# Maximum tiles paced by VectorE's work, one PSUM pool, first weights in pieces, and an output projection in program order

## The chip, the cores and the metric

The kernel runs on one core of one Trainium2 chip. The metric is device microseconds of one execution; the median of three runs of the kernel before is 1812.08 us. The engines are called as the profile calls them: PE (TensorE matmuls), PEld (its weight loads), DVE (VectorE), ACT (ScalarE), POOL (GpSimd), SP (SyncE, which issues DMAs).

## The reference

The kernel mixes, by a gate for each token, an attention block and a token-mixing MLP on the same input x of 2048 tokens and 640 channels:

```
q, k, v = split(x @ wqkv)                      # 32 heads of 20
a = softmax(q k^T / sqrt(20)) v  @ wo          # 2048 x 640
h = layernorm(x)                               # over channels
u = gelu(h^T @ w1 + b1)                        # 640 x 1728, over tokens
b = (u @ w2 + b2)^T                            # 2048 x 640
g = sigmoid(sum(x * gate_w, -1))
out = g * a + (1 - g) * b
```

All is float32. Products are made of a high part rounded for the fast matmul and a low part (`hi_lo`), three matmuls for one.

## The kernel before

The work is one program in five stages.

1. **q and k projections** (0 to 63 us). `qk_unit(m, w, q)` makes one tile of 128 output channels by 512 tokens with 15 matmuls into one PSUM tile and then evacuates it: the high part by ACT (`evh`), the low part by DVE (`evl`), and for some units a third copy by DVE (`kf`). The first weights (`wr0`) come in one DMA on ACT's queue, x in twenty pieces on SP's.
2. **v projections** (63 to 134 us), 32 units of 15 matmuls, evacuated by ACT (`vt`) and, in the first half, by DVE (`gs`, which also feeds the gate). Then the other q and k units (134 to 218 us), beside the splitting of the normalised rows (`h_split`) and loads of the next weight tile: at the first of a weight tile's four units ACT issues the load of the next one and, in its own order, waits for it in `load_w`.
3. **Token MLP** (218 to 746 us): `mlp` is a generator of 2592 steps, each one or two matmuls into a pair of half-width tiles. Beside its steps runs the **maximum stream**: for the softmax, the largest score of each query row is needed ahead of the exponentials, so all scores are made once with PE and only their maxima kept. For the first 8 head pairs (`s_diff`) halves of the keys are differenced, so that ACT (relu, `ov`) and DVE (`tensor_tensor_reduce`) share the work; for the rest (`s_raw`) DVE alone reduces every tile (`mx`). The stream takes 1082 tiles beside the MLP (1024 differenced, 58 raw), two at a time, spread evenly over the steps; what is left runs in the attention loop.
4. **Attention loop** (747 to 1721 us): 512 iterations, each with scores (`st`), exponentials on ACT (`p`) and the product with v on PE (`pv`). Its output `o_d` and the softmax sums `l_d` go to DRAM; `norm_steps` loads the sums, takes reciprocals on DVE and stores them, broadcast, to `r_d`.
5. **Output projection** (1722 to 1800 us): for each of 16 row tiles 24 matmuls over four of the five channel chunks, then in a second pass six matmuls for the last chunk, each pass evacuated by DVE into `oy`, which already holds the MLP's part.

The order on PE, and in stages 1 to 4 on ACT and DVE (from the MLP on also on POOL and SP), is the program's own order. In the output projection of the kernel before, only PE's order is fixed by the program (`ordered.close()` stands ahead of it); the other engines' is the scheduler's. In the MLP a small planner (`act`, `later_on`, `settle`, `force`) sets where ACT's work stands: each piece has a cost, a delay and a slack, and the earliest due comes first.

**PSUM** has 8 banks: the pool `four` (later `trio`, then `late`) gives four tiles in rotation (`st0` to `st3`) to `st_tile`, which the projections, the MLP and the output projection use; the rest belong to the maximum stream (`s`, `s3`, `pv`). In the attention loop the scores take one two-bank tile (`two`) and single ones (`one0`, `one1`, `s3`).

Of the kernel before, what the change touches and what calls it, by code (L numbers as in the profile page):

```python
# [10 lines left out]
OP = mybir.AluOpType  # L11
# [19 lines left out]
def gated_mix(ctx, tc, xT, x, wqk, wv0, wv1, wo, w1, w1t, b1, w2, b2, out):  # L31
# [303 lines left out]

    def load_x(q):
        for c in range(NC):
            raw = px.tile([P, 512], F32, tag="x", bufs=8, name=f"xr{c}_{q}")
            nc.sync.dma_start(raw, xT[c * P:(c + 1) * P, q * 512:(q + 1) * 512])
            hi_lo(xh[c][q], xl[c][q], raw, hi_eng=nc.scalar)  # L340
# [453 lines left out]

    def norm(h0, h1, at):
        loads, recips, stores = norm_steps(h0, h1)
        for n, f in enumerate(loads + recips + stores):
            if at is None:
                f()
            else:  # L800
                later[at if n == 0 else at + 10 + 2 * n] = f

    def pv_evac(p, qh, pv):
        ev = ap.tile([P, 512], F32, tag="oev", bufs=2, name=f"oev{p}_{qh}")
        nc.vector.tensor_copy(ev, pv)  # L805
        for j in range(2):
            h = 2 * p + j
            for c in range(2):
                r = 32 * (2 * j + c) + 11 * j
                cols = slice(qh * 1024 + c * 512, qh * 1024 + (c + 1) * 512)  # L810
                nc.gpsimd.dma_start(o_d[DH * h: DH * h + DH, cols], ev[r: r + DH, :])  # L811
                nc.gpsimd.dma_start(l_d[h: h + 1, cols], ev[r + DH: r + DH + 1, :])
        if qh == 1 and p in (7, 11, 13, 15):
            norm({7: 0, 11: 16, 13: 24, 15: 28}[p], 2 * p + 2, None if p == NP - 1 else 32 * p + 38)
# [23 lines left out]
    o_hl = {}  # L838

    def o_part(q, rows, k, n, tag, bufs, hi_eng, lo_eng):  # L840
        def t(name, dt=F32):
            return ap.tile([P, k, n], dt, tag=name + tag, bufs=bufs, name=f"{name}{tag}{q}")
        raw, rb, oh, ol = t("or"), t("rb"), t("oh", F32R), t("ol", F32R)
        cols = slice(q * n, (q + 1) * n)
        nc.sync.dma_start(raw, o_d[rows].rearrange("(c p) s -> p c s", p=P)[:, :, cols])
        nc.sync.dma_start(rb, r_v[rows].rearrange("(c p) s -> p c s", p=P)[:, :, cols])
        nc.vector.tensor_mul(raw, raw, rb)
        hi_lo(oh, ol, raw, hi_eng=hi_eng, lo_eng=lo_eng)
        return [(oh[:, i], ol[:, i]) for i in range(k)]

    def o_early(q, hi_eng=nc.scalar, lo_eng=nc.vector):
        o_hl[q] = o_part(q, slice(0, (NC - 1) * P), NC - 1, 256, "e", 2, hi_eng, lo_eng)

    def o_late(q):
        return o_part(q, slice((NC - 1) * P, D), 1, 512, "l", 4, nc.scalar, nc.vector)[0]
# [11 lines left out]
    def st_pair(g):  # L867
        ps = tp.tile([P, 2, 512], F32, tag="two", bufs=1, name=f"st{g}_0")
# [6 lines left out]
    def st_one(g, j):  # L875
        n = (2 * g + j) % 3
        ps = (psum if n == 2 else tp).tile([P, 512], F32, tag=("one0", "one1", "s3")[n], bufs=1, name=f"st{g}_1{j}")
# [6 lines left out]
    for p in range(NP):  # L884
# [3 lines left out]
        for it in range(32):  # L888
# [14 lines left out]
            if p == NP - 1 and it in (20, 26):  # L903
                o_early(it // 26, nc.gpsimd, nc.gpsimd)
# [25 lines left out]
    def a_mms(t, ps, ohl, cc, cs):  # L930
        passes = [z for k, (oh, ol) in zip(cs, ohl) for z in ((oh[:, cc], woh[k]), (oh[:, cc], wol[k]),
                                                              (ol[:, cc], woh[k]))]
# [4 lines left out]
        c = slice(t, t + 1)  # L937
        for i in range(2):
            nc.vector.scalar_tensor_tensor(tys[t][:, i], ps[i], g_t[:, c], tys[t][:, i], op0=OP.mult, op1=OP.add)  # L939

    last = []
# [59 lines left out]
```

## Time and profile before

| | |
|---|---|
| runs | 1811.72, 1812.08, 1812.80 us |
| profiled execution, own time | 1807.24 us |
| its span | 1804.9 us |
| PE busy | 1787.0 us (99%), 14978 matmuls |
| ACT busy | 1483.9 us (82%) |
| DVE busy | 1240.6 us (69%) |
| POOL busy | 641.8 us (36%) |
| mean granted PE clock | 0.997 |

The profile comes from one execution, so its rows are set against its own time of 1807.24 us, which is 4.84 us below the median of the runs. A row of the windows table gives a stretch of the span, the busy time and number of instructions of each engine in it, the granted clock and the DMA traffic. A row of the timeline gives start, duration, engine, line, operation, the names of output and inputs, and in brackets the idle time before it and what ended that. A row of the table of waits gives the total, the number and the longest. A row of the groups of instructions gives busy time, mean duration in ns, and idle time ahead.

### The profile page before, as it was taken

Reading aid. Unit: us, or ns where it says so; the run is one execution under the profiler, and the core shown is the slowest. Engines: PE = TensorE matmul, PEld = TensorE weight load, DVE = VectorE, ACT = ScalarE, POOL = GpSimd, SP = SyncE. Lnnn points to the kernel's source line nnn. Section 1 sums busy time; section 2 is a strip of 40 time slices with the busy share of each in tenths; the row PEclk is TensorE's granted clock in tenths of the full one; section 3 lists DMA queues with packets and bytes.
Section 4 is the critical chain, followed back from the end, with each engine's and each line's share of the span. In section 5 each row is a group of like instructions: output and inputs, shape, how many; then the busy total and the mean of one; then the engine's idle time right before and its main releaser. Section 6 shows DMA issues by size and latency. Waiting matters only on the chain. (4 is left out here: it accounts for less than half of the span.)

```text
span 1804.9 us, 39919 instructions
## 1 busy us (share of the span) xinstructions
PE 1787.0 (99%) x14978; PEld 1117.5 (62%) x14978; DVE 1240.6 (69%) x2407; ACT 1483.9 (82%) x2535; POOL 641.8 (36%) x898
## 2 busy tenths in 40 slices
PE   9999999999999999999999999999999999999998
PEld 7998799999999999533333333333333333333378
DVE  5303288899988888877767767676767677766136
ACT  4244378887888887699999999999999999999920
POOL 2113378788877777211110211121322121212210
PEclk9999999999999999999999999999999999999999
DMA  8657866556675564225222232052353332301463
GB/s 301 233 172 247 269 160 170 160 160 190 187 182 149 156 178 141 70 59 135 59 53 58 62 90 61 18 113 62 62 122 69 72 71 53 73 14 23 134 223 135
DMA packets 155666, 222.96 MB, mean 124 GB/s; under 512 B 65998, under 2 KB 92382, under 8 KB 152046
## 3 DMA queue, kind: packets, MB, share of 16 engines
q1 hardware_dynamic: 135472, 186.78, 38.2%
q0 software_dynamic: 15104, 23.01, 5.4%
q10 hardware_dynamic: 4896, 10.62, 1.8%
q8 instruction: 118, 1.93, 0.5%
q14 instruction: 76, 0.62, 0.1%
HBM read 165.43 MB, written 54.54 MB: 122 GB/s over the span
## 5 line engine op out<-in xcount | busy, mean ns | idle before, releaser
L205 DVE TENSOR_REDUCE mx<-s 128x1 f32<-128x512 f32 x1280 | 833.7, 687 | 288.9 <-PE s L199 225.1
L880 ACT ACTIVATE p<-st 128x512 f32<-128x512 f32 x1024 | 585.1, 659 | 0.0
L872 ACT ACTIVATE p<-st 128x1024 f32<-128x1024 f32 x512 | 553.8, 1082 | 1.3 <-PE st L865 0.7
L824 PE MATMUL pv<-p,v 128*32 128x512 f32 x4096 | 548.5, 605 | 0.1
L865 PEld LDWEIGHTS st<-qs_True,ks_True 62*128 62x128 f32 x2048 | 246.2, 185 | 434.9 <-ACT p L872 428.7
L865 PE MATMUL st<-qs_True,ks_True 62*128 62x512 f32 x2048 | 495.7, 446 | 1.8 <-ACT x L587 1.1
L199 PE MATMUL s<-ks_False,qs_False 60*128 60x512 f32 x1152 | 391.0, 398 | 4.5 <-ACT ov L214 2.9
L43 POOL TENSOR_TENSOR wl<-wr,wh 128x512 fp32r<-128x512 f32 x228 | 275.4, 1217 | 89.0 <-ACT wh L40 66.8
L224 DVE CUSTOM_DVE_ANT_0 ov<-s,ov 128x512 f32<-128x512 f32 x384 | 263.4, 687 | 38.6 <-PE s L199 24.9
L214 ACT ACTIVATE ov<-s 128x512 f32<-128x512 f32 x384 | 228.7, 597 | 73.0 <-PE s L199 61.9
L199 PE MATMUL s<-sk,sq 60*128 60x512 f32 x896 | 279.9, 394 | 0.0
L811 POOL DMA_DIRECT2D o_d<-oev x128 | 66.6, 521 | 590.4 <-DVE oev L805 587.9
L48 PE MATMUL y<-gh,wh 64*128 64x320 f32 x896 | 225.0, 309 | 0.0
L48 PE MATMUL u<-hl,wh 64*128 64x320 f32 x864 | 224.7, 307 | 0.0
L48 PE MATMUL u<-hh,wh 64*128 64x320 f32 x864 | 224.5, 307 | 0.0
L199 PEld LDWEIGHTS s<-ks_False,qs_False 60*128 60x128 f32 x1152 | 211.2, 185 | 14.7 <-DVE mx L205 6.7
L48 PE MATMUL y<-gl,wh 64*128 64x320 f32 x832 | 216.7, 307 | 0.0
L48 PE MATMUL y<-gh,wl 64*128 64x320 f32 x832 | 215.3, 306 | 0.0
L48 PE MATMUL u<-hh,wl 64*128 64x320 f32 x800 | 212.3, 307 | 0.0
L824 PEld LDWEIGHTS pv<-p,v 128*32 128x32 f32 x4096 | 83.1, 108 | 175.1 <-issue 162.6
L40 ACT ACTIVATE wh<-wr 128x512 fp32r<-128x512 f32 (+2 forms) x246 | 146.9, 600 | 52.7 <-DMA wr<-in_wqk_dram 22.5
L199 PEld LDWEIGHTS s<-sk,sq 60*128 60x128 f32 x896 | 166.3, 186 | 18.0
(130 smaller groups left out, 2441.3 us busy)
## 6 DMA issues: line engine op xcount, KB each, us to landing
wr<-in_w_dram SPq DMA_DIRECT2D x192, 256.0 KB
ks_True<-k_d SPq DMA_DIRECT2D x96, 160.0 KB
qs_True<-q_d SPq DMA_DIRECT2D x192, 80.0 KB
qs_False<-q_d SPq DMA_DIRECT2D x108, 80.0 KB
sk<-k_d SPq DMA_DIRECT2D x42, 160.0 KB
sq<-q_d SPq DMA_DIRECT2D x84, 80.0 KB
v_d<-vt SPq DMA_DIRECT2D x32, 168.0 KB
v<-v_d SPq DMA_DIRECT2D x16, 336.0 KB
```

The lines of the kernel that those rows point to most:

```text
L40: nc.scalar.activation(hi, src, AF.Copy)
L43: (lo_eng or nc.vector).tensor_sub(lo, src, hi.bitcast(F32))
L48: nc.tensor.matmul(ps[k], a[r], b[r], start=start, stop=stop)
L199: nc.tensor.matmul(ps, qs[half][r, t * P:(t + 1) * P], ks[r, kc * 512:(kc + 1) * 512], start=True, stop=True)
L205: nc.vector.tensor_reduce(mx[:, slot, j, t: t + 1], ps, axis=AX.X, op=OP.max)
L214: nc.scalar.activation(over[j, kc], ps, AF.Relu)
L224: nc.vector.tensor_tensor_reduce(ov, ps, ov, 1.0, -3.0e38, OP.add, OP.max, mx[:, slot, j, t: t + 1])
L811: nc.gpsimd.dma_start(o_d[DH * h: DH * h + DH, cols], ev[r: r + DH, :])
L824: nc.tensor.matmul(pv[r: r + 32, :], v_tiles[p][:, kt, 10 * j: 10 * j + 32], pt[j, c], start=(kt == 0), stop=(kt == NT - 1))
L865: nc.tensor.matmul(ps, ks[r, kt * P:(kt + 1) * P], qs[qh][r, c * 512:(c + 1) * 512], start=True, stop=True)
L872: nc.scalar.activation(pt, ps, AF.Exp, scale=SCALE)
L880: nc.scalar.activation(pt, ps, AF.Exp, scale=SCALE)
```

## The change

- `st_tile` gives the two halves of one two-bank tile (`two`) for every first and second call of four, and two single tiles (`one0`, `one1`) for the third and fourth. All PSUM tiles now come from one pool, and `four`, `trio` and `late` are gone, so the attention loop's tiles are the same as the earlier stages'.
- The warm-up takes 8 matmuls in another tile. The first weights come in five DMAs, all x loads of the first column are issued at once, and the splits of weights and x alternate.
- The maximum stream is paced by an estimate of DVE's work: 435 for a differenced tile, 640 for a raw one, 400 for each row tile that DVE normalises in the second half of the channels, from step 14 on. The splits of the first 8 weight chunks of the MLP have another delay and slack.
- The softmax sums are stored ahead of the outputs; the last normalisation's reciprocals and stores are placed in the output projection.
- The output projection is written in program order for all engines (`ordered.close()` at the end). From row tile 8 on, a tile takes all five chunks at once, and behind it stands the last chunk of the tile 8 rows earlier.

The core of the diff:

```diff
-    four = ExitStack()
-    banks = [four.enter_context(tc.tile_pool(name="four", bufs=1, space=PSUM))]
 
     def st_tile(shape, name):
         n = st_count[0] % 4
         st_count[0] += 1
-        return banks[0].tile(shape, F32, tag=f"st{n}", bufs=1, name=name)
+        if n == 0:
+            st_pair_of[0] = psum.tile([P, 2, 512], F32, tag="two", bufs=1, name=name)
+        if n < 2:
+            return st_pair_of[0][:, n, :shape[1]]
+        return psum.tile(shape, F32, tag=f"one{n - 2}", bufs=1, name=name)
...
-    wps = st_tile([P, 512], "warm_ps")
-    for i in range(10):
-        nc.tensor.matmul(wps, warm[:, :P], warm, start=(i == 0), stop=(i == 9))
-    raws = {0: w_dma(0), NC: w_dma(NC)}
-    w = {0: load_w(0, raws[0])}
-    load_x(0)
+    wps = s3_tile([P, 512], "warm_ps")
+    for i in range(8):
+        nc.tensor.matmul(wps, warm[:, :P], warm, start=(i == 0), stop=(i == 7))
+    wr0 = p1.tile([P, NC, P], F32, tag="xr", bufs=2, name="wr0")
+    for c in range(NC):
+        nc.scalar.dma_start(wr0[:, c], wqk[0][:, c])
+    xr0 = [x_dma(c, 0) for c in range(NC)]
+    raws = {NC: w_dma(NC)}
+    w = {0: tuple(q4([P, NC, P], F32R, f"w{n}0") for n in "hl")}
+    for c in range(NC):
+        hi_lo(w[0][0][:, c], w[0][1][:, c], wr0[:, c], hi_eng=nc.scalar)
+        x_split(c, 0, xr0[c])
...
-            act(lambda: w_split(j), 520, 0, 2200 * (j - k) - 4000)
+            act(lambda: w_split(j), 520, 4000 if j < 2 * AHEAD else 0, 2000 if j < 2 * AHEAD else 2200 * (j - k) - 4000)
...
+    FIRST = 14
+    U_STEPS = (FT - 1) * 48 + 32
+    DIFF, RAW, NORM = 435, 640, 400
+
+    def dve_work(k):
+        return DIFF * min(k, NDIFF * 128) + RAW * max(0, k - NDIFF * 128)
+
+    def dve_room(n):
+        norms = min(max((n - U_STEPS) / (NT * 40), 0), 1) * NT * NORM
+        return (dve_work(S_AHEAD) + NT * NORM) * (n + 1 - FIRST) / (STEPS - FIRST) - norms
...
-        while done + 2 <= S_AHEAD and done < S_AHEAD * (n + 1) / STEPS:
+        while done + 2 <= S_AHEAD and dve_work(done) < dve_room(n):
...
-    four.close()
-    trio = ExitStack()
-    tp = trio.enter_context(tc.tile_pool(name="trio", bufs=1, space=PSUM))
...
         if qh == 1 and p in (7, 11, 13, 15):
-            norm({7: 0, 11: 16, 13: 24, 15: 28}[p], 2 * p + 2, None if p == NP - 1 else 32 * p + 38)
+            h0 = {7: 0, 11: 16, 13: 24, 15: 28}[p]
+            if p == NP - 1:
+                last_norm.extend(norm_steps(h0, H))
+                last_norm[0][0]()
+            else:
+                norm(h0, 2 * p + 2, 32 * p + 38)
...
     pv_flush()
-    ordered.close()
     lps.close()
-    trio.close()
-    banks[0] = ctx.enter_context(tc.tile_pool(name="late", bufs=1, space=PSUM))
...
     for t in range(NT):
-        if t % 2 == 0 and t // 2 + 2 < NT // 2:
-            o_early(t // 2 + 2)
-        nc.sync.dma_start(tys[t].rearrange("p a b -> p (a b)"), y_d[t * P:(t + 1) * P, :])
-        if t in (4, 6, 8, 10):
-            last.append(o_late(t // 2 - 2))
-        ps = [st_tile([P, HALF], f"a{t}_{i}") for i in range(2)]
-        a_mms(t, ps, o_hl[t // 2], slice((t % 2) * P, (t % 2 + 1) * P), range(NC - 1))
-    for t in range(NT):
-        ps = [st_tile([P, HALF], f"b{t}_{i}") for i in range(2)]
-        a_mms(t, ps, [last[t // 4]], slice((t % 4) * P, (t % 4 + 1) * P), [NC - 1])
-        nc.scalar.dma_start(out[t * P:(t + 1) * P, :], tys[t].rearrange("p a b -> p (a b)"))
+        q = t // 2 + 2
+        if t % 2 == 0 and 2 < q < NT // 2:
+            e_high(q, ap if q % 4 < 2 else ep)
+        if t == 2:
+            for f in last_norm[2]:
+                f()
+            for n in (2, 0, 3, 1):
+                l_load(n)
+        for n in {NT // 2 - 2: (2, 0), NT // 2 + 1: (3, 1)}.get(t, ()):
+            l_high(n)
+        evacs = [a_tile(t, range(NC) if t >= NT // 2 else range(NC - 1))]
+        if t >= NT // 2:
+            evacs.append(a_tile(t - NT // 2, [NC - 1]))
...
+        for f in evacs:
+            f()
+        if t == 1:
+            for f in last_norm[1]:
+                f()
+    ordered.close()
```

How this moves instructions shows at three places. The first is PE's order where the first unit with the weights of m = 1 ends and its second begins. A row names the output tile, then the moving and the stationary operand; the number behind a name is the buffer's. Before:

```order
L54 MATMUL qk1_0_489<-xh4_0_117,wh1_351 128x512
L54 MATMUL qk1_0_489<-xl4_0_137,wh1_351 128x512
L54 MATMUL qk1_0_489<-xh4_0_117,wl1_352 128x512
L54 MATMUL qk1_1_515<-xh0_1_102,wh1_351 128x512
L54 MATMUL qk1_1_515<-xl0_1_122,wh1_351 128x512
L54 MATMUL qk1_1_515<-xh0_1_102,wl1_352 128x512
```

and in the changed kernel, at the same place:

```order
L54 MATMUL qk1_0_494<-xh4_0_114,wh1_357 128x512
L54 MATMUL qk1_0_494<-xl4_0_134,wh1_357 128x512
L54 MATMUL qk1_0_494<-xh4_0_114,wl1_358 128x512
L54 MATMUL qk1_0_494<-xh0_1_99,wh1_357 128x512
L54 MATMUL qk1_0_494<-xl0_1_119,wh1_357 128x512
L54 MATMUL qk1_0_494<-xh0_1_99,wl1_358 128x512
```

The order of the matmuls is the same; the second unit's output was a tile of its own and is now the same tile as the first unit's (its other half).

The second is ACT's order where the MLP begins: `wh` and `wtmp` are the high parts of MLP weight chunks, `wr` their raw loads, `ov` the relu of a differenced tile `s`. Before:

```order
L40 ACTIVATE evh_3_2174<-qk_3_2158 128x512
L40 ACTIVATE wtmp_1447<-wr_2128 128x512
L483 DMA wr_2188<-in_w_dram 128x512
L483 DMA wr_2190<-in_w_dram 128x512
L40 ACTIVATE wh_2196<-wr_2154 128x512
L214 ACTIVATE ov_0_0_1_0_2205<-s_0_0_1_0_2201 128x512
L214 ACTIVATE ov_0_0_1_2_2220<-s_0_0_1_2_2213 128x512
```

and now:

```order
L40 ACTIVATE evh_3_2163<-qk_3_2147 128x512
L40 ACTIVATE wtmp_1442<-wr_2117 128x512
L499 DMA wr_2176<-in_w_dram 128x512
L499 DMA wr_2178<-in_w_dram 128x512
L218 ACTIVATE ov_0_0_1_0_2219<-s_0_0_1_0_2215 128x512
L218 ACTIVATE ov_0_0_1_2_2234<-s_0_0_1_2_2227 128x512
L40 ACTIVATE wh_2244<-wr_2143 128x512
```

The split of the chunk that follows stood ahead of the first two relus and now stands behind them.

The third is PE's order near the MLP's end, among the raw maximum tiles `s`; `y` rows are the MLP's own matmuls, and `x2` marks two of them in one row. Before:

```order
L199 MATMUL s_0_4_1_0_13332<-ks_False,qs_False_11652 128x512
L199 MATMUL s_0_4_0_0_13335<-ks_False,qs_False_11652 128x512
L48 MATMUL y_14_0_13248<-gh_7_9786,wl_13139 128x320
L48 MATMUL y_14_1_13249<-gh_7_9786,wl_13139 128x320
L48 MATMUL y_14_0_13248<-gh_8_9986,wh_13180 128x320
L48 MATMUL y_14_1_13249<-gh_8_9986,wh_13180 128x320
L48 MATMUL y_14_0_13248<-gl_8_9987,wh_13180 128x320
L48 MATMUL y_14_1_13249<-gl_8_9987,wh_13180 128x320
L48 MATMUL y_14_0_13248<-gh_8_9986,wl_13181 128x320
L48 MATMUL y_14_1_13249<-gh_8_9986,wl_13181 128x320
L48 MATMUL y_14_0_13248<-gh_9_10186,wh_13180 128x320
L48 MATMUL y_14_1_13249<-gh_9_10186,wh_13180 128x320
```

and now, up to the next pair of tiles:

```order
L203 MATMUL s_0_4_1_0_13231<-ks_False,qs_False_11496 128x512
L203 MATMUL s_0_4_0_0_13234<-ks_False,qs_False_11496 128x512
L48 MATMUL y_14_0_13238<-gh_0_8147,wh_13095 128x320 x2
L48 MATMUL y_14_0_13238<-gl_0_8148,wh_13095 128x320 x2
L48 MATMUL y_14_0_13238<-gh_0_8147,wl_13096 128x320 x2
L48 MATMUL y_14_0_13238<-gh_1_8372,wh_13095 128x320 x2
L48 MATMUL y_14_0_13238<-gl_1_8373,wh_13095 128x320 x2
L48 MATMUL y_14_0_13238<-gh_1_8372,wl_13096 128x320 x2
L203 MATMUL s_0_4_1_1_13256<-ks_False,qs_False_11496 128x512
L203 MATMUL s_0_4_0_1_13259<-ks_False,qs_False_11496 128x512
```

Ten MLP matmuls stood between two pairs of raw tiles before, twelve (at other places fourteen) stand there now.

More of the change, by code (lines that the diff above doesn't have):

```diff
@@ L793, in gated_mix @@
     later = {}
+    last_norm = []
     def norm(h0, h1, at):
@@ L805, in pv_evac @@
         nc.vector.tensor_copy(ev, pv)
+        stores = []
         for j in range(2):
@@ L851, in o_early, with o_tiles, o_load @@
[L851 to L855, printed above, removed]
+    o_raw, o_hl, l_hl = {}, {}, {}
+    def o_tiles(q, k, n, tag, bufs, names, pool, dt):
+        return [pool.tile([P, k, n], dt, tag=name + tag, bufs=bufs, name=f"{name}{tag}{q}") for name in names]
+    def o_load(q, rows, k, n, tag, bufs, eng):
+        raw, rb = o_tiles(q, k, n, tag, bufs, ("or", "rb"), ap, F32)
+        cols = slice(q * n, (q + 1) * n)
+        for dst, src in ((raw, o_d[rows]), (rb, r_v[rows])):
+            eng.dma_start(dst, src.rearrange("(c p) s -> p c s", p=P)[:, :, cols])
+        o_raw[q, tag] = raw, rb
@@ L867, in st_pair @@
     def st_pair(g):
-        ps = tp.tile([P, 2, 512], F32, tag="two", bufs=1, name=f"st{g}_0")
+        ps = psum.tile([P, 2, 512], F32, tag="two", bufs=1, name=f"st{g}_0")
         for j in range(2):
@@ L876, in st_one @@
         n = (2 * g + j) % 3
-        ps = (psum if n == 2 else tp).tile([P, 512], F32, tag=("one0", "one1", "s3")[n], bufs=1, name=f"st{g}_1{j}")
+        ps = psum.tile([P, 512], F32, tag=("one0", "one1", "s3")[n], bufs=1, name=f"st{g}_1{j}")
         st_mm(g, j, 1, ps)
@@ new lines, in a_tile, with y_load @@
+        return evac
+    def y_load(t):
+        nc.sync.dma_start(tys[t].rearrange("p a b -> p (a b)"), y_d[t * P:(t + 1) * P, :])
+    for t in range(6):
+        y_load(t)
+    e_high(2, ep)
+    for t in range(NT):
+        q = t // 2 + 2
[11 more added lines that the diff above has]
+            evacs.append(a_tile(t - NT // 2, [NC - 1]))
+        if t % 2 == 0 and q < NT // 2:
+            e_low(q)
+            if q + 2 < NT // 2:
+                e_load(q + 2)
+        if t + 6 < NT:
+            y_load(t + 6)
+        for n in {NT // 2 - 2: (2, 0), NT // 2 + 1: (3, 1)}.get(t, ()):
+            l_low(n)
+        for f in evacs:
[3 more added lines that the diff above has]
+                f()
```

82 lines of the change are left out of this document (56 added, 26 removed).

## Prediction

> **What bounds the kernel now.** I read the page's busy line first, then the windows table for stage after stage, then the table of waits, and last the timeline of single units where a wait would arise.
>
> ```profile
> span 1804.9 us, 39919 instructions
> PE 1787.0 (99%) x14978; PEld 1117.5 (62%) x14978; DVE 1240.6 (69%) x2407; ACT 1483.9 (82%) x2535; POOL 641.8 (36%) x898
> ```
>
> PE is busy 1787.0 of 1804.9 us, so outside the attention loop time can be won only where PE idles, or where it is busy at a slower pitch; and any new wait of PE adds to the end. Attention (747 to 1721 us) is paced by the exponentials on ACT, which the change leaves alone.
>
> ```profile
> 50.00:100.00 50.00, 50.00 (x307) 47.58 (x306) 13.02 (x35) 13.81 (x31) 6.27 (x23) 1.00 0.57 191
> 300.00:350.00 50.00, 50.00 (x617) 49.85 (x615) 43.66 (x112) 42.76 (x83) 38.60 (x41) 1.00 0.49 144
> 400.00:450.00 50.00, 49.60 (x596) 48.08 (x595) 46.34 (x114) 39.86 (x80) 40.15 (x45) 1.00 0.68 189
> 220.00:224.00 4.00, 1.15 (x12) 0.81 (x10) 1.52 (x3) 2.28 (x5) 2.04 (x2) 1.00 0.92 332
> 224.00:228.00 4.00, 4.00 (x34) 4.00 (x32) 2.46 (x7) 1.83 (x4) 1.78 (x2) 0.58 0.98 310
> 228.00:232.00 4.00, 4.00 (x53) 4.00 (x51) 3.14 (x7) 2.83 (x5) 2.48 (x2) 0.99 0.92 224
> 705.00:710.00 5.00, 5.00 (x65) 4.96 (x64) 4.26 (x12) 3.94 (x9) 3.08 (x3) 1.00 0.58 185
> 715.00:720.00 5.00, 4.89 (x53) 4.05 (x51) 5.00 (x10) 2.56 (x5) 3.47 (x7) 1.00 0.34 102
> 740.00:745.00 5.00, 4.90 (x50) 3.93 (x50) 5.00 (x9) 0.00 (x0) 0.00 (x0) 1.00 0.01 3
> 1745.00:1750.00 5.00, 3.40 (x24) 3.14 (x22) 1.57 (x2) 0.73 (x1) 0.00 (x0) 1.00 0.91 315
> 1750.00:1755.00 5.00, 4.80 (x21) 4.55 (x22) 2.63 (x5) 0.00 (x0) 0.00 (x0) 0.66 0.87 292
> 1755.00:1760.00 5.00, 5.00 (x35) 4.91 (x35) 4.13 (x6) 1.06 (x1) 0.00 (x0) 1.00 0.46 150
> ```
>
> The columns are the window's length, then busy time and (count) of PE, weight loads, DVE, ACT, POOL, then the granted clock, DMA share and GB/s. While q, k and v are projected, PE never idles (50.00 of 50). In the token MLP it runs 617 matmuls in 50 us, 0.081 us each. It idles at the MLP's start and is then granted 0.58. Near the MLP's end DVE is full (5.00 of 5) and PE's count falls from 65 to 53 and 50: the pace of the raw maxima. In the output projection it idles and is then granted 0.66.
>
> ```profile
> PE a L935 <- DVE oy L939: 3.0, 2, 1.8
> PE s L199 <- ACT ov L214: 2.9, 1, 2.9
> ACT wh L40 <- DMA wr<-in_wqk_dram: 22.5, 6, 5.5
> DVE rl L785 <- DMA rl<-l_d: 5.2, 1, 5.2
> ```
>
> These are total, times and longest. PE's waits are few; ACT's wait for the next weight tile, up to 5.5 us, costs nothing yet, because PE writes to three other PSUM tiles meanwhile.
>
> **The change, part by part. The shared pair.** Where four PSUM tiles stood, `st_tile` now gives two halves of one tile, then two single tiles. A unit of the q, k and v projections takes one tile at a time and is evacuated as soon as it is done. The unit in the second half writes to the same tile that the unit in the first half has still to be evacuated from, so its first matmul waits for that evacuation (in PE's order it is the same tile name, for `qk1_0` and `qk1_1`). In the MLP and the output projection both halves are filled and evacuated together, so there it costs nothing. The first unit's matmul of a pair waits for nothing new. Of 72 units every fourth opens a pair: 18 boundaries, 10 in qk units, 8 in v units. What PE then loses is the lag, the end of a unit's last evacuation less the start of the next unit, which the timeline of before shows.
>
> ```profile
> 39.37 0.39 PE L54 MATMUL qk<-xh,wh 128*128 128x512 f32 x1
> 39.62 0.60 ACT L40 ACTIVATE evh<-qk 128x512 fp32r<-128x512 f32 x1 [0.90 <-PE qk L54]
> 40.25 0.69 DVE L43 TENSOR_TENSOR evl<-qk,evh 128x512 fp32r<-128x512 f32 x1 [0.81 <-ACT evh L40]
> 74.54 0.46 PE L54 MATMUL v<-wv,xh 128*128 128x322 f32 x2
> 74.87 0.44 ACT L422 ACTIVATE vt<-v 128x320 f32<-128x320 f32 x1 [1.44 <-PE v L54]
> 75.34 0.16 DVE L425 COPY gs<-v 128x2 f32<-128x2 f32 x1 [1.39 <-ACT vt L422]
> ```
>
> The floor, where ACT and DVE are free, is 40.94 − 39.37 = 1.57 us for a qk unit (about 2.1 where a third evacuation follows, another 0.69 us on DVE less its pipelined start), 75.50 − 74.54 = 0.96 for a v unit of the first half and, without the last row, 75.31 − 74.54 = 0.77 for the second half. Elsewhere ACT is late:
>
> ```profile
> 11.91 0.39 PE L54 MATMUL qk<-xh,wh 128*128 128x512 f32 x1
> 14.85 0.69 DVE L43 TENSOR_TENSOR evl<-qk,evh 128x512 fp32r<-128x512 f32 x1
> 127.70 0.46 PE L54 MATMUL v<-wv,xh 128*128 128x320 f32 x2
> 130.83 0.42 ACT L422 ACTIVATE vt<-v 128x320 f32<-128x320 f32 x1
> 137.80 0.40 PE L54 MATMUL qk<-xh,wh 128*128 128x512 f32 x1
> 141.09 1.07 ACT L40 ACTIVATE evh<-qk 128x512 fp32r<-128x512 f32 x2
> 141.96 1.28 DVE L43 TENSOR_TENSOR evl<-qk,evh 128x512 fp32r<-128x512 f32 x2
> 177.40 0.34 ACTq L286 DMA_DIRECT2D wr<-in_wqk_dram  x1
> 179.80 0.40 PE L54 MATMUL qk<-xh,wh 128*128 128x512 f32 x1
> 182.99 0.74 ACT L40 ACTIVATE wh<-wr 128x640 fp32r<-128x640 f32 x1 [5.01 <-DMA wr<-in_wqk_dram]
> 184.60 0.69 DVE L43 TENSOR_TENSOR evl<-qk,evh 128x512 fp32r<-128x512 f32 x1
> 207.80 0.40 PE L54 MATMUL qk<-xh,wh 128*128 128x512 f32 x1
> 212.86 0.69 DVE L43 TENSOR_TENSOR evl<-qk,evh 128x512 fp32r<-128x512 f32 x1 [1.95 <-DMA q_d<-evl]
> ```
>
> The lags are 15.54 − 11.91 = 3.63 for the first boundary, 131.25 − 127.70 = 3.55 for the last v one, 142.65 − 137.80 = 4.85 (the first of the two evacuations ends at 141.96 + 0.69) after a chain of small ACT work, 185.29 − 179.80 = 5.5 where ACT waits for the next weight tile, and 213.55 − 207.80 = 5.75 for the last boundary. All 18 read so sum to 59.5 us. Not every lag comes back whole: a stalled PE gives DMAs more time. Four classes: six v boundaries at their floors, 5.2. Two qk boundaries at theirs (the third of this kind traced 4.87, but ACT was then behind x loads that PE's stalls let finish), 3.1. Four where the next weight tile is awaited: the tile is issued and awaited at the same place of ACT's order, so its 5.6 us from issue to use stay as long as the DMAs are loaded; traced 3.33, 6.14, 5.50 and 6.78, of which I take 3.1, 4.4, 3.8, 4.2 for lighter traffic, 15.5. Six of other causes, traced 3.63, 3.56, 4.73, 3.55, 4.84, 5.75; I take 3.4, 2.5, 3.8, 3.55, 4.85, 2.2 (those that hang on stores still in flight are cut), 20.3. Together 44.1 us; bounds 34 (DMA-bound lags near half) and 59.5.
>
> Nothing covers these waits: behind the waiting matmul stands all of PE's program. After an idle PE the clock is lowered too. The 4 us window after the 2.85 us idle ran 34 matmuls where the next ran 53, 4 × (1 − 34/53) = 1.43 us lost; after the 1.8 us idle in the output projection the clock was 0.66 and the 5 us held 21 and not 35 rows. I charge 1.43 to each of the ten stalls of about 1.8 us or more: 14.3 (bounds 8.6 for six, 17 for twelve). The Trainium skill, "TensorE: Matmul & The Clock Gate", under "Why this matters for your kernels", says that only PE gaps above about 3 us drop the clock, to half. By that rule eight stalls pay and the term is 11.4; the 0.66 after 1.8 us here speaks against it, so the row decides. Loss: 44.1 + 14.3 = 58.4.
>
> **The MLP's start.** The maximum stream now begins 14 steps in, and the first weight splits come later in ACT's order: the split that waited for its DMA at 222.51 no longer stands ahead of the relu that PE awaited. That gives back 2.85 and its 1.43: 4.3.
>
> **Pacing by VectorE's work.** The budget is 435 × 1024 + 640 × 58 + 400 × 16 = 488,960 units over 2592 − 14 = 2578 steps, 189.7 a step: 0.436 matmuls a step for the differenced maxima, 0.296 for raw ones, where before both ran at 1082/2592 = 0.417.
>
> ```profile
> L205 DVE TENSOR_REDUCE mx<-s 128x1 f32<-128x512 f32 x53 | 31.8, 684 | 0.0
> ```
>
> In the last 31 us of the MLP, DVE was without a gap: a reduce every 0.6 us, a pair every 1.2. Now a pair comes every 6.75 steps, 13.5 MLP matmuls and its own two, 15.5 × 0.081 = 1.26 us on PE: DVE just keeps up. PE lost there about 30 − 315/13 = 5.8 us (315 matmuls in the six windows from 715 to 745, each between 50 and 54; 13 a us by the row at 705); I take 6.0, bounds 3 and 6. Around 350 to 500 us, where DVE normalises the second half's rows, windows held 596 to 610 instead of 617, 3.3 us in all, but the stream is slowed only from 0.417 to 0.413 there: 0.5, bounds 0 and 3.3. Elsewhere it is denser: −0.5.
>
> **The seam and the output projection.**
>
> ```profile
> 747.11 0.73 PE L865 MATMUL st<-qs_True,ks_True 62*128 62x512 f32 x3 [1.12 <-ACT x L587]
> ```
>
> The wait for the closed pool's last reader goes, but the loop's first pair still needs its own tile: 0.7 (0 to 1.1). In the output projection the two waits (3.0), their slow clock (1.4) may go; but everything now stands in program order: DVE's reciprocal waits for its load (5.2 before) with the evacuations of later row tiles queued behind it, and in the second half a row tile of 30 matmuls is followed by six of another, 6 × 5.00/35 = 0.86 us, while its two evacuations take about 1.4 (six took 4.13 in the window at 1755): some 0.5 us of wait, eight times, an estimate of 4 against the 4.4 gained. I take 0, bounds ±4.4. Loads issued in pieces at the start shorten the first wait at most a little, and are in the first boundary's 3.4.
>
> **Sum.** Gains 4.3 + 6.0 + 0.5 − 0.5 + 0.7 + 0 = 11.0, bounds 3 and 19. Net +58.4 − 11.0 = +47.4. The profiled execution took 1807.24 us, 4.84 below the median 1812.08; the sum is a difference, so I add it to the median: 1859.5, say 1859.
>
> **The rivals.** *Only the floors* (15%): the weight waits come from queued traffic that the stalls let drain. Then the boundaries that hang on a DMA fall to 1.6 to 2.1 (or the v floors), 28.6 in all with four clock drops (5.7): +34.3 − 11.0 = +23, 1835. For it: landing times grow with the DMA share. Against: the wait of 5.01 us follows right on its issue. *The lags in full* (12%): 59.5 + 17 − 11.0 = +65.5, 1877. *Pacing does not help* (5%): the raw tail stays, +6, 1865. *The other side* (3%): the evacuation of one half runs beside the next unit's matmuls in the other half, as the four tiles did; PE waits at no boundary and only the gains are left, with up to 1.5 us of the start: −12.5, 1799.6. It decides at one place, whether the first matmul into the second half waits. The Trainium skill, "Perfetto Trace Analysis", under "Matmuls", has independent groups rotate through PSUM banks so that the evacuation of one overlaps the next; the halves are two banks, so by that rule alone this rival would hold. Against it is PE's order, where both units have one tile's name and the wait is for the tile. *Nothing to see* (2%): floors of 23 us without clock losses against upper gains of 19, about 1815.
>
> **How the numbers follow.** Forecast 63%: 1859. Its own ends are 34 + 8.6 − 19 = +24 and 59.5 + 17 − 3 = +73, both taken together unlikely. The range 1832 to 1880 takes in the forecast's middle, the full lags and most of the floors case. What a measurement can tell from no change is 0.2%, 3.6 us. Faster 0.03, same 0.02, slower 0.95.
>
> **What would show it.** In the profile after: waits of PE qk and v on DVE evl, DVE kf, DVE gs and ACT vt, 18 of them, 34 to 60 us; PE below 50 in the windows up to 220 us and clocks under 1 behind the long ones; the windows near the MLP's end at 62 to 65 matmuls; no 2.85 us wait at its start. I am wrong if those 18 waits are absent, under 25 us in sum, or if the attention loop's length changes.

## The result, and the profile after

The changed kernel took 1871.51 us (median of six runs, 1867.54 to 1875.88) against 1812.44 us for the kernel before beside it: a ratio of 1.0325, 95% interval 1.0306 to 1.0343. It is 59 us slower; the forecast was +47. The profiled execution took 1867.54 us.

The page's first lines, then PE's part of the table of waits (total, times, longest), of the changed kernel:

```profile
span 1865.6 us, 39904 instructions
PE 1799.2 (96%) x14976; PEld 1116.7 (60%) x14976; DVE 1233.1 (66%) x2395; ACT 1482.5 (79%) x2539; POOL 643.7 (35%) x906
```

```profile
PE qk L54 <- DVE evl L43: 30.0, 8, 6.3
PE a L995 <- DVE oy L1001: 8.1, 9, 4.6
PE v L54 <- ACT vt L438: 7.1, 4, 5.1
PE v L54 <- DVE gs L441: 5.5, 4, 2.9
PE qk L54 <- DVE kf L321: 5.3, 2, 3.3
```

The four rows on `qk` and `v` hold 8 + 4 + 4 + 2 = 18 waits and 47.9 us. None of them stood in the profile before. The longest one, with the evacuation that ends it (first the evacuation, then the first matmul of the unit in the other half):

```profile
215.42 0.69 DVE L43 TENSOR_TENSOR evl<-qk,evh 128x512 fp32r<-128x512 f32 x1
216.17 0.80 PE L54 MATMUL qk<-xh,wh 128*128 128x512 f32 x1 [6.25 <-DVE evl L43]
```

At all 18 boundaries the timeline has this: the second unit's first matmul starts 0.05 to 0.06 us after the last evacuation of the first unit ends. The windows table shows what is left of the projections' full PE (a 50 of 50 before), the granted clock under 1 (third number from the end), and the other side, the MLP's end, where a window of 5 us now holds 67 matmuls instead of 50 to 54 (62 to 65 were forecast):

```profile
50.00:100.00 50.00, 42.75 (x211) 36.78 (x210) 15.40 (x31) 12.49 (x26) 9.28 (x24) 0.97 0.72 235
150.00:200.00 50.00, 36.87 (x175) 31.63 (x174) 7.47 (x14) 18.50 (x38) 7.54 (x15) 0.93 0.46 138
771.00:776.00 5.00, 5.00 (x67) 4.96 (x65) 5.00 (x11) 2.61 (x5) 4.45 (x5) 1.00 0.68 185
796.00:801.00 5.00, 5.00 (x67) 5.00 (x65) 5.00 (x9) 1.72 (x3) 0.88 (x1) 1.00 0.10 36
```

Cutting the span where the first matmul of each stage starts (from the timeline) gives the length of each stage in us, each from the one profiled execution of its run. The runs of the next section are in the same table:

| | projections | MLP | attention | output | tail | median of runs, ratio to before |
|---|---|---|---|---|---|---|
| before | 211.4 | 528.7 | 974.6 | 77.9 | 5.3 | |
| changed | 278.4 | 516.8 | 975.8 | 83.4 | 4.4 | 1871.5, 1.0325 |
| 1 four tiles | 212.9 | 520.3 | 976.2 | 81.8 | 4.2 | 1807.2, 0.9978 |
| 2 pair only | 274.8 | 522.6 | 975.5 | 79.5 | 4.5 | 1867.0, 1.0313 |
| 3 first try | 305.5 | 515.8 | 975.8 | 85.5 | 4.4 | 1896.2, 1.0475 |
| 3 filled | 262.5 | 517.2 | 975.8 | 84.3 | 4.4 | 1853.3, 1.0222 |
| 4 pacing only | 211.8 | 524.8 | 974.9 | 75.8 | 5.0 | 1801.7, 0.9950 |
| 5 reciprocals later | 278.5 | 517.6 | 975.9 | 85.5 | 4.4 | 1868.2, 1.0296 |
| 6 idle tiles | 213.2 | 520.3 | 975.8 | 84.7 | 4.4 | 1806.7, 0.9962 |
| 7 alternating | 228.3 | 515.6 | 975.6 | 84.0 | 4.4 | 1822.6, 1.0041 |
| 8 old output | 210.9 | 521.0 | 975.8 | 78.1 | 4.7 | 1801.4, 0.9947 |
| 9 start at 44 | 212.4 | 529.1 | 975.5 | 80.0 | 4.2 | 1806.3, 0.9970 |

The changed kernel lost 67.0 in the projections, 5.5 in the output projection and 1.2 in attention, and won 11.9 in the MLP and 0.9 in the tail. One part of this is only where the cut falls: in the runs with one pool the attention loop's first matmul starts 0.48 us before the MLP's last one ends, in the others 1.1 us after it. Counted to the end of the MLP's last matmul, the MLP won 10.4 us (527.6 to 517.2), and attention from there on took 975.7 us before and 975.3 after.

### The profile page after: what moved, and what is told of

The parts are those of the page before. It is cut to its first block, busy times and chain, and to the rows that moved or that the text cites. A ratio compares the mean times of both kernels' runs of the same rounds, so it can differ in the third digit from the quotient of the medians.

```text
span 1865.6 us, 39904 instructions
## 1 busy us (share of the span) xinstructions
PE 1799.2 (96%) x14976; PEld 1116.7 (60%) x14976; DVE 1233.1 (66%) x2395; ACT 1482.5 (79%) x2539; POOL 643.7 (35%) x906
## 4 chain that ended last, share of the span: by engine, by line
PE 89%; DMA 4%; issue 3%; DVE 2%; ACT 1%; POOL 1%; SPq 0%; ACTq 0%; DVEq 0%; POOLq 0%
PE pv L855 27%; PE st L920 20%; PE s L203 12%; PE u L48 10%; PE y L48 9%; PE qk L54 4%; PE v L54 4%; PE a L995 2%; DMA wr<-in_wqk_dram 1%; DMA kd_d<-kf 1%; DVE oy L1001 1%; DVE evl L43 0%; DMA wr<-in_w_dram 0%; DMA rbl<-r_d 0%; DVE ov L228 0%
## 5 line engine op out<-in xcount | busy, mean ns | idle before, releaser
L935 ACT ACTIVATE p<-st 128x512 f32<-128x512 f32 x1024 | 567.7, 625 | 0.0
L927 ACT ACTIVATE p<-st 128x1024 f32<-128x1024 f32 x512 | 536.7, 1048 | 0.7 <-PE st L920 0.7
L203 PE MATMUL s<-ks_False,qs_False 60*128 60x512 f32 x1152 | 336.6, 396 | 1.5 <-ACT ov L218 0.8
L218 ACT ACTIVATE ov<-s 128x512 f32<-128x512 f32 x384 | 227.9, 597 | 66.1 <-PE s L203 60.6
L835 POOL DMA_DIRECT2D l_d<-oev x128 | 62.5, 495 | 594.6 <-DVE oev L828 591.9
L48 PE MATMUL y<-gh,wl 64*128 64x320 f32 x832 | 212.9, 305 | 0.0
L203 PEld LDWEIGHTS s<-ks_False,qs_False 60*128 60x128 f32 x1152 | 189.1, 184 | 6.1 <-DVE mx L228 1.5
L40 ACT ACTIVATE wh<-wr 128x512 fp32r<-128x512 f32 (+3 forms) x250 | 147.8, 594 | 52.4 <-DMA wr<-in_wqk_dram 20.4
L48 PE MATMUL u<-hl,wh 64*128 64x320 f32 x864 | 177.0, 307 | 0.0
L48 PE MATMUL u<-hh,wh 64*128 64x320 f32 x864 | 177.0, 307 | 0.0
L203 PEld LDWEIGHTS s<-sk,sq 60*128 60x128 f32 x896 | 166.1, 186 | 17.8
L48 PE MATMUL u<-hh,wl 64*128 64x320 f32 x800 | 165.4, 307 | 0.0
```

What stands on the lines that cost most here:

```text
L40: nc.scalar.activation(hi, src, AF.Copy)
L48: nc.tensor.matmul(ps[k], a[r], b[r], start=start, stop=stop)
L203: nc.tensor.matmul(ps, qs[half][r, t * P:(t + 1) * P], ks[r, kc * 512:(kc + 1) * 512], start=True, stop=True)
L218: nc.scalar.activation(over[j, kc], ps, AF.Relu)
L927: nc.scalar.activation(pt, ps, AF.Exp, scale=SCALE)
L935: nc.scalar.activation(pt, ps, AF.Exp, scale=SCALE)
```

## The experiments

**1. Four tiles again in the changed kernel.**

```diff
-        if n == 0:
-            st_pair_of[0] = psum.tile([P, 2, 512], F32, tag="two", bufs=1, name=name)
-        if n < 2:
-            return st_pair_of[0][:, n, :shape[1]]
-        return psum.tile(shape, F32, tag=f"one{n - 2}", bufs=1, name=name)
+        return banks[0].tile(shape, F32, tag=f"st{n}", bufs=1, name=name)
...
+    four.close()
+    trio = ExitStack()
...
+    banks[0] = ctx.enter_context(tc.tile_pool(name="late", bufs=1, space=PSUM))
```

> The changed kernel with only its PSUM edit undone: four separate tiles in rotation (pools four, trio, late) instead of the shared pair, all other edits kept. In the changed kernel's trace the projections took 278.4 us, 66.9 more than before; the MLP took 12.0 less, the output projection 5.5 more, the attention loop 1.2 more. Theory (the shared tile makes PE wait): the 18 waits of PE on evl, kf, gs and vt go, the projections fall back to 211 us, and the time is 1812 - 12 + 5.5 + 1 = about 1807 us. Rival (the first weights in pieces, the x loads issued at once and the alternating splits slow the projections): they stay above 240 us and the time above 1835.

Measured: 1807.2 us, ratio 0.9978 (0.9963 to 0.9992), projections 212.9. The rows of the same two windows:

```profile
50.00:100.00 50.00, 49.67 (x299) 46.78 (x299) 13.41 (x35) 13.29 (x31) 6.18 (x22) 1.00 0.58 199
150.00:200.00 50.00, 50.00 (x216) 40.51 (x215) 15.23 (x22) 15.84 (x31) 20.08 (x26) 1.00 0.86 270
```

PE is full again, as the theory had it. All but 1.5 us of the loss in the projections goes with the shared tile; the rest is the most that the other edits of the first stage cost.

**2. Only the pair, in the kernel before** (and one pool in place of `four`, `trio` and `late`).

```diff
-        return banks[0].tile(shape, F32, tag=f"st{n}", bufs=1, name=name)
+        if n == 0:
+            st_pair_of[0] = psum.tile([P, 2, 512], F32, tag="two", bufs=1, name=name)
+        if n < 2:
+            return st_pair_of[0][:, n, :shape[1]]
+        return psum.tile(shape, F32, tag=f"one{n - 2}", bufs=1, name=name)
...
-    wps = st_tile([P, 512], "warm_ps")
+    wps = s3_tile([P, 512], "warm_ps")
```

> The kernel before with only the PSUM edit: one pool, and the first two of every four tiles are halves of one (the warm-up goes to another tile, as in the changed kernel, so that the pairs fall alike). Theory: the projections alone carry the loss, +67 us within 5, nothing is gained elsewhere: about 1879 us, above the changed kernel's 1871. Rival (it takes the other edits as well): less than half of it, below 1846.

Measured: 1867.0 us, ratio 1.0313 (1.0278 to 1.0347): nearly all of the loss, with no other edit. The projections lost 63.4, within the 67 and 5 of the theory; but the MLP won 6.1, which was not expected. The evacuations of the MLP's tiles, counted from its first matmul, are ahead of the kernel before by 4.53 us at the first tile and by 4.5 at the last: that gain is all at the start, and the 1.6 us beyond it are where the cut falls. At the start the wait of 2.85 us is gone:

```profile
281.78:285.78 4.00, 4.00 (x46) 3.81 (x47) 2.48 (x5) 3.73 (x7) 2.57 (x2) 1.00 1.06 286
798.55:803.55 5.00, 4.89 (x51) 3.78 (x47) 5.00 (x10) 0.00 (x0) 0.00 (x0) 1.00 0.01 4
```

The first row is the MLP's first 4 us, without idle time and at full clock; the last is its end, where DVE is still the limit, as before. The order of ACT at that place is the old one. So the stalled projections themselves remove the wait at the MLP's start: ACT begins the projections' last evacuation 0.1 us after the MLP's first matmul, and had begun it 1.3 us after it in the kernel before.

**3. The waits filled.** The fill is an accumulation that nothing reads.

```diff
+        k = FILL.get(name, 0)
+        fill = s3_tile([P, 512], "fill") if k else None
+        for i in range(k):
+            nc.tensor.matmul(fill, xh[0][0][:, :P], xh[0][0], start=(i == 0), stop=(i == k - 1))
...
+    FILL = {"qk5_0": 14, "qk5_2": 17, "qk6_1": 7, "v0_1": 11, "v1_13": 20, "qk2_1": 19, "qk7_1": 13,
+            "qk3_1": 25, "qk8_1": 10, "qk4_1": 22}
```

In a first try each filling matmul had a tile of its own:

> The changed kernel with matmuls of no use (0.23 us each, into a bank that the projections leave idle) put ahead of the first matmul of the ten units that waited 1.8 us or more, 7 to 25 of them, as many as the wait seen there holds; they are extra work and the waits stay. Theory (of the 66.9 us lost some 48 are waits and some 17 the lower clock after them): the waits count as busy now, the granted clock goes from 0.988 to about 0.996, and the time falls by 10 to 17 us, to about 1857. Rival (the rest of the loss is something else, or the clock follows the waits in the mean and not the gaps): no change or slower, 1871 or more.

That one took 1896.2 us, ratio 1.0475 (1.0448 to 1.0501), since each matmul waited for the one ahead: the timeline's first group is 14 of them in 7.68 us, 0.55 us each, so that the fill outlasted the waits.

```profile
12.61 7.68 PE L77 MATMUL fill<-xh 128*128 128x512 f32 x14
```

But with the gaps filled no clock drop was left in its projections (mean clock of the execution 0.998). With one accumulation:

> The filling matmuls again, now as one accumulation in one tile, since in the first try each waited for the one ahead of it (0.53 us each, 84 us in all where the waits hold some 43). 158 of them at 0.233 us are 36.8 us, less than the waits that they stand in. Theory (part of the loss is the lower clock behind an idle PE): the granted clock of 0.988 rises to about 0.997 and the time falls by 10 to 17 us, to about 1857. Rival (the clock costs nothing that counts, because ACT and DMAs set the pace of the projections then): less than 4 us.

Measured: 1853.3 us, ratio 1.0222 (1.0207 to 1.0238), 18 us less than the changed kernel, as the theory had it; mean clock 0.998. The windows of the projections, clock third from the end (0.97 and 0.93 in the changed kernel):

```profile
50.00:100.00 50.00, 47.45 (x247) 41.40 (x248) 14.40 (x30) 11.93 (x26) 7.48 (x21) 1.00 0.68 220
150.00:200.00 50.00, 49.59 (x235) 41.53 (x234) 11.95 (x21) 19.02 (x37) 9.36 (x15) 1.00 0.52 165
```

The projections took 262.5 against 278.4, 15.9 less, though 158 useless matmuls were added. Of these, 14.7 lie within the eight units that ran behind a clock drop in the changed kernel (1.4 to 3.0 each, from first matmul to the next unit's), and that is the price of the clock; the rest are somewhat shorter waits.

**4. Only the pacing, in the kernel before.**

```diff
-        while done + 2 <= S_AHEAD and done < S_AHEAD * (n + 1) / STEPS:
+        while done + 2 <= S_AHEAD and dve_work(done) < dve_room(n):
...
-            act(lambda: w_split(j), 520, 0, 2200 * (j - k) - 4000)
+            act(lambda: w_split(j), 520, 4000 if j < 2 * AHEAD else 0, 2000 if j < 2 * AHEAD else 2200 * (j - k) - 4000)
```

> The kernel before with only the pacing edit (budget by VectorE's work, start at step 14, later first weight splits). Theory: all of the MLP's gain is this edit's, 12 us within 2, so about 1800 us; the 2.85 us wait at its start goes and the last 30 us hold 62 to 65 matmuls in 5 us. Rival (part of the gain is the one PSUM pool's, or comes of the later and calmer start of the MLP in the changed kernel): under 6 us, above 1806.

Measured: 1801.7 us, ratio 0.9950 (0.9931 to 0.9969); the time is the theory's, but the MLP is shorter by 3.9 us, not by 12, which is the rival's. Another 2.1 lie in the output projection, where the edit does nothing, and about 3 are in no stage of the table: the medians differ by 9.4, the two profiled executions by 6.0. The end of the MLP is repaired as in the changed kernel; its start is not. At the first evacuated tile the run is 0.03 us ahead of before. ACT's row of the timeline there:

```profile
223.74 0.60 ACT L40 ACTIVATE evh<-qk 128x512 fp32r<-128x512 f32 x1 [2.16 <-DMA k_d<-evh]
225.87 1.09 ACT L214 ACTIVATE ov<-s 128x512 f32<-128x512 f32 x2 [1.02 <-DMA k_d<-evl]
226.52 0.50 PE L199 MATMUL s<-ks_False,qs_False 60*128 60x512 f32 x1 [2.05 <-ACT ov L214]
```

The MLP began at 218.88, but ACT still evacuates the last unit of the projections at 223.74, after a wait for its buffer to be stored. The relu that PE waits for stands behind that, whatever the order of the weight splits. So moving the split did not take the wait away here. It is not the same in every run: in 1, which has this edit too and no stalls, ACT began the last evacuation 2.0 us after the MLP's first matmul, not 4.9, and 3.3 us were won at the first evacuated tile.

**5. Reciprocals one row tile later, in the changed kernel.**

```diff
-        if t == 2:
+        if t == 3:
             for f in last_norm[2]:
...
-        if t == 1:
+        if t == 2:
             for f in last_norm[1]:
```

The expectation speaks of this place of the changed kernel, DVE's and PE's timeline there:

```profile
1791.74 0.55 DVE L809 RECIPROCAL rl<-rl 128x64 f32<-128x64 f32 x1 [5.72 <-DMA rl<-l_d]
1796.79 0.87 PE L995 MATMUL a<-woh,ohe 128*128 128x320 f32 x2 [4.63 <-DVE oy L1001]
```

> The changed kernel with the last normalisation's reciprocals and its stores one row tile later in the output projection (behind the evacuation of row tile 2, stores at 3). There DVE waited 5.72 us for the sums to land, with the evacuation of row tile 2 queued behind; PE waited 4.63 us for that and ran at a clock of 0.59 to 0.73 after it. Theory: the wait of 4.63 goes with its clock, 6 us faster, about 1865. Rival (the chain from the sums to the last chunk's factors is late anyway, so that the wait moves to the row tiles that need them): under 2 us.

Measured: 1868.2 us, ratio 1.0296 (1.0278 to 1.0314), an interval that overlaps the changed kernel's (3.4 us less by the medians, so the time decides between neither); its output projection took 85.5 against 83.4. The rival held for the wait, which moved: the 4.63 is gone, and one wait of 8.59 stands at row tile 8, the first that needs the last chunk:

```profile
1808.56 0.69 DVE L884 TENSOR_TENSOR orl<-orl,rbl 128x512 f32<-128x512 f32 x1 [6.21 <-DMA rbl<-r_d]
1815.94 0.87 PE L995 MATMUL a<-woh,ohe 128*128 128x320 f32 x2 [8.59 <-DVE oy L1001]
```

The last chunk's factors (`rbl`) land 30 us after the output projection's first matmul at 1778.9. Eight row tiles of four chunks are some 28 us of PE; sixteen, as in the kernel before, are 56.

**6. Six idle tiles for the projections, reciprocals later, in the changed kernel.**

```diff
+    def unit_tile(shape, name):
+        tag = UNIT_TAGS[unit_count[0] % len(UNIT_TAGS)]
+        unit_count[0] += 1
+        return psum.tile(shape, F32, tag=tag, bufs=2 if tag == "s" else 1, name=name)
+    unit_count, UNIT_TAGS = [0], ("s", "one0", "s", "one1", "s3", "pv")
...
-    ps = st_tile([P, 512], f"qk{m}_{q}")
+    ps = unit_tile([P, 512], f"qk{m}_{q}")
...
-            ps = st_tile([P, width], f"v{half}_{t}")
+            ps = unit_tile([P, width], f"v{half}_{t}")
```

> A version to beat both: as the one with the reciprocals later, and the projections' units rotate over six single tiles that lie idle then (s, s, s3, pv of the maximum stream, one0 and one1), none of them half of a pair. Theory: the projections take 211 to 213 us as with four tiles; the MLP gains 8 to 9; the output projection is within 1 of before: 1812 - 9 + 1 + 1 = about 1804. Rival (the maximum stream's tiles now wait for the last units' evacuations at the MLP's start, and the reciprocals' wait moves): 1810 or more.

Measured: 1806.7 us, ratio 0.9962 (0.9947 to 0.9977). The projections lost their waits with one pool kept (213.2), as the theory had it. The rival's two waits came as well: PE waited 1.8 us at the MLP's start for an evacuation of the last units, and the output projection (84.7, not within 1 of before) kept a wait of 8.1 us.

**7. The pair's halves apart: half, single, half, single.**

```diff
-        n = st_count[0] % 4
+        n = (0, 2, 1, 3)[st_count[0] % 4] if alternate[0] else st_count[0] % 4
```

> The changed kernel with the rotation in the projections as half, single, half, single, so that one unit of 3.5 us (2.2 for v) lies between the two that share a tile. Theory (the wait is for the shared tile, as long as the evacuation lags): waits shorten by one unit each; those of 0.8 to 1.6 us vanish, of the long ones 8 to 25 us stay in sum, and the time is 1812 to 1836, about 1824. Rival (the wait is for any evacuation, whichever tile): the sum stays above 40 us and the time above 1860.

Measured: 1822.6 us, ratio 1.0041 (1.0024 to 1.0058). PE's waits on the projections' evacuations fall to 5.7 + 2.1 + 1.0 us in 6 waits, the longest 2.2, and the 0.8 us waits are gone. A further 3.6 us ahead of a `v` matmul has no releaser in the table; it ends 0.1 us after DVE's `kf` copy of the pair's last half, two units earlier, so it may be a wait of the same kind. Together that is 12.4 us, within the 8 to 25 of the theory: the wait is the lag beyond what lies between the two units that share a tile.

**8. The old output projection with the pacing, one pool and the idle tiles** (the kernel before with 4's edit and 6's `unit_tile`).

> The kernel before with the pacing edit, one pool, and the projections' units on six idle single tiles; its output projection is that of before (two passes over the row tiles, the last chunk in the second), the first weights come as before. Theory (the output projection in program order loses because the last chunk's factors, which land some 33 us after its start, are needed after 8 row tiles and not after 16): the projections take 211 to 213 us, the MLP 520 to 524, the output projection 76 to 79 instead of 84.7, the time is 1799 to 1803. Rival (the run with pacing alone was faster for another reason, four tiles and later pools): 1806 or more, as the version with the new output projection.

Measured: 1801.4 us, ratio 0.9947 (0.9933 to 0.9960), output projection 78.1, all as the theory had it. It is the lowest ratio of all, level with 4; both beat the kernel before and the changed one. The edit takes back the program order and the single pass together, so it does not say what each of them costs.

**9. The same with the stream's start at step 44** (`FIRST = 44`).

> The same with the maximum stream's start at step 44 instead of 14. At step 14 the relu that PE waits for stands in ACT's order behind the last evacuations of the projections, which wait for their stores (ACT was some 5 us behind PE there). Theory: the waits on the relu (2 us and less) go, 1 to 3 us faster than the run beside it. Rival (PE then waits at the same time for the MLP's own weight chunks, whose splits stand in the same order behind the same evacuations): no change within 1 us.

Measured: 1806.3 us, ratio 0.9970 (0.9958 to 0.9982): 4.9 us slower than 8 by the medians, which neither had. The profiled execution was the slowest of nine (1810.2), and that of 8 the fastest of five (1799.3), so the stages differ by more than that. The wait on the relu did not go but grew, and the MLP took 529.1:

```profile
224.55 0.41 PE L48 MATMUL u<-hh,wtmp 64*128 64x320 f32 x2 [1.20 <-ACT wtmp L40]
235.03 0.63 ACT L40 ACTIVATE wh<-wr 128x512 fp32r<-128x512 f32 x1 [4.29 <-DMA wr<-in_w_dram]
236.20 0.80 PE L210 MATMUL s<-ks_False,qs_False 60*128 60x512 f32 x2 [4.29 <-ACT ov L225]
```

PE now also waits for the MLP's own weights, the rival's wait. The relu is late because a weight split stands ahead of it in ACT's order again, and that split waited 4.29 us for its load.

## Why the prediction came out right

The slower time, the 18 waits and the clock behind them came as forecast. The spans of the two profiled executions differ by 60.6 us where the forecast was 47.4. Of the 13 missing, 5.5 are the output projection, 4.4 are parts of the projections that the forecast put at nothing, and 3.8 are the waits; the other terms miss by 1.1 or less each and nearly cancel.

**The shared pair: right, and the largest term.** The 18 boundaries are there, 47.9 us by the table of waits where 44.1 were forecast. By class:

- The six v boundaries at their floors: 5.2 forecast, 4.6 measured. They are 0.86 and 0.66 each, since an idle time begins at the last matmul's end, 0.1 to 0.2 us after the point where the forecast's lag began.
- The two qk boundaries at their floors: 3.1 forecast, measured 1.46 and 4.31.
- The four with a weight wait: 15.5 forecast, 17.8 measured. Single ones missed by up to 1.9 us (4.4 forecast, 6.25 measured), so part of the sum is luck.
- The other six: 20.3 forecast, 19.8 measured.

The step that failed is the excuse for the traced 4.87, the second boundary in time, which came back nearly whole as 4.31. The x loads did land earlier: ACT waits for none of them there, where it had waited 0.72 us before. But ACT's own work stands ahead of the evacuation (`evh`), behind a wait for DVE:

```profile
30.97 0.63 ACT L40 ACTIVATE dh<-kf 128x512 fp32r<-128x512 f32 x1 [1.35 <-DVE kf L327]
31.51 2.69 ACT L40 ACTIVATE xh<-xr 128x512 fp32r<-128x512 f32 x5
34.11 0.72 ACT L40 ACTIVATE wh<-wr 128x640 fp32r<-128x640 f32 x1
34.74 0.57 ACT L40 ACTIVATE evh<-qk 128x512 fp32r<-128x512 f32 x1
```

Experiments 1 and 2 show the cause from both sides, 7 its size. Of the 67.0 us, 47.9 are these waits and 14.7 the clock (experiment 3). The 4.4 left had no term in the forecast: 2.6 for the last matmul's end at the 18 boundaries (0.10 to 0.16 each, not counted as idle), 1.2 for the first unit, whose 15 matmuls spanned 6.3 us where they had spanned 5.0 before, and small amounts at the first matmul behind each wait.

**The clock: right in sum, wrong in its rule.** Forecast ten drops of 1.43, 14.3 us; there were eight in the projections, 14.7 us in sum. The failing step is "about 1.8 us or more": after 2.01 us (at 69.80) and 3.29 us (at 195.90) nothing dropped, after 2.74 (at 235.48) it did. The windows of 3 us behind these three gaps, granted clock third from the end:

```profile
69.80:72.80 3.00, 3.00 (x13) 2.49 (x14) 0.35 (x1) 0.00 (x0) 0.00 (x0) 1.00 0.78 246
195.90:198.90 3.00, 2.99 (x13) 2.49 (x14) 0.00 (x0) 0.46 (x1) 1.47 (x2) 1.00 0.61 164
235.48:238.48 3.00, 3.00 (x7) 2.42 (x8) 0.00 (x0) 0.47 (x1) 2.01 (x3) 0.50 0.82 244
```

In all traces of this case, every gap of 3.6 us or more dropped the clock, and gaps from 1.77 to 3.29 us went either way (run numbers in brackets). Dropped after short ones: 1.77 (before), 1.83 (8), 2.05 (4), 2.26 (9), 2.54 (5). Not dropped: 2.01 (changed), 2.43 (7), 2.88 (2 and 5), 3.29 (changed). What decides between them is open. The Trainium skill, "TensorE: Matmul & The Clock Gate", "Why this matters for your kernels", has a clock of one half after gaps above about 3 us. The clock of 0.50 agrees; the limit of about 3 us does not hold sharply here. That the prediction counted eight stalls by that rule, as many as dropped, is in part luck: seven of its eight dropped, the 3.29 did not, and the 4.31 that it had at a floor did.

**The MLP's start: right size, the cause only in part.** Forecast 4.3 from the later split; the gain was 5.4 us at the first evacuated tile. But the pair alone, with the old order of the splits, gave 4.5 (2). Without the stalls the pacing edit gave from nothing to 3.3: 0.03 (4), 1.2 (8), 2.1 (6) and 3.3 (1). ACT's backlog goes some way with this. It began the projections' last evacuation 4.9, 5.3, 5.0 and 2.0 us after the MLP's first matmul in these four, and 0.1 us after it where the projections stalled (changed, 2). Why it is so far behind in some runs without stalls is open. So the stalls are enough for most of this gain, and part of it was paid for by the change's largest loss.

**The pacing: right in direction, both terms too small.** In the changed kernel the last three evacuated tiles of the MLP win 8.1 us (forecast 6.0), and the denser stream ahead of them loses 3.2 (forecast 0.5 − 0.5 = 0). With the old pacing (2) nothing was lost there. The net is 4.9 where 6.0 was forecast. Experiment 4 has it at 3.9: ahead of the kernel before by 0.03 at the first tile, behind it by 4.2 before the last three, ahead by 3.9 at the end.

**The output projection: wrong by 5.5.** The wait of DVE on its reciprocal, with the evacuations behind it, was named and came (5.72, and 4.63 for PE), as did seven waits of 0.2 to 0.3 where eight of 0.5 were taken, and one of 1.70 that was not foreseen. But that wait on the reciprocal was given no price: the 4 us of cost were the short waits alone, against 4.4 gained. PE's waits came to 8.1 us where 3.0 had stood, and the clock dropped behind the 4.63 as it had behind the 1.77 before. The last chunk is needed after 8 row tiles, 28 us, and arrives after 30 to 33, so taking the reciprocal away from its place only moves the wait, from 4.63 to 8.59 (5, and 8.1 in 6). Over all runs the five output projections in two passes took 75.8 to 80.0 us (before, 2, 4, 8, 9) and the seven in program order 81.8 to 85.5.

**The seam and attention.** The first wait at the seam fell from 1.12 to 0.48, 0.6 against the forecast 0.7. The attention loop's 1.2 us more are where the cut falls (see the result): from the end of the MLP's last matmul it took 0.4 us less than before, so this sign of being wrong, a changed length of the loop, is absent.

**The other cases.** Only the floors: wrong, of the long lags just two fell to their floors, the last (1.41) and the one of 3.56 that hung on a third evacuation (2.01). The lags in full: the measured +59 lies between it (+65) and the forecast (+47), but not because the lags came back whole; 5.5 of the difference is the output projection. The other side: PE waited at all 18 boundaries, though the two halves lie in different banks. That it waits, and for which evacuation, is measured; that the built order asks for the whole tile is what experiments 1, 2, 6 and 7 agree on. The rule on rotating banks (the Trainium skill, "Perfetto Trace Analysis", "Matmuls"), taken alone, did not hold here.

## What to carry to other kernels

In these kernels a PSUM tile of two banks was one thing to whoever waited for it: give its halves to work that is filled and evacuated together, and to units that are evacuated one by one give tiles of their own, or put at least one unit between the halves. When a wait of the critical engine is to be priced, read the lag of the evacuation at that very unit, not the floor, and add the clock in full for gaps that always dropped it in your traces (3.6 us and more here) and as a range for the shorter ones. Before a late result is moved forward in an order, count how much work stands ahead of its first use and set it against the time at which it lands.

## What the runs showed that was not expected

A stall early in a kernel paid 4.5 us back later (2): while PE waited, ACT caught up, and the next stage began without its wait. Matmuls of 128x512 that write, each as its own start, to one bank through tiles of their own ran at 0.55 us where an accumulation of the same runs at 0.23.
